# Splitting two more middle branches in a strided convolution's forward, with shared branch sums and a two-instruction cube term

## The chip, the cores and the metric

The kernel runs on one core of one Trainium2 chip. The time is that of one execution on the device, in microseconds (us). Of the kernel before there are three timed runs, 1151.36, 1152.18 and 1155.96 us (median 1152.18), and one execution taken by the profiler. TensorE (PE) multiplies matrices; its results stand in PSUM. VectorE (DVE) and ScalarE (ACT) work element by element, POOL does small copies and fills, and SP issues most transfers. Each engine works through its own queue in order.

## What is computed

```python
B, T, D, K = 2, 16000, 256, 31
s = 2
L = (T - K) // s + 1            # 7985
h = jnp.einsum('blc,cd->bld', x[:, 0:s * L:s, :], w[0])
for i in range(1, K):
    h = h + jnp.einsum('blc,cd->bld', x[:, i:i + s * L:s, :], w[i])
mu = jnp.einsum('bld->bd', h)[:, None, :] / L
var = jnp.einsum('bld->bd', (h - mu) ** 2)[:, None, :] / L
h = (h - mu) / jnp.sqrt(var + 1e-5)
h = h * gn_gamma[None, None, :] + gn_beta[None, None, :]
return _gelu(h)
```

The kernel returns this output and the gradients of `x`, `w`, `gn_gamma` and `gn_beta` for a given `grad_out`. Inputs and outputs are bfloat16.

## The kernel before

The convolution of 31 taps and stride 2 is split by phases. At each level two phase sequences and their sum replace products, so that there are three products where plain work has four. The first level has the **branches** A, B_ (the middle one) and C_, done in the order `ORDER = (B_, A, C_)`; each branch has the **leaves** A, B_ and C_ again; and the third level splits a leaf once more. A leaf can be done in two ways. `f_leaf` does it without the third split, in 24 (or 20) matmuls for each half `dh` of the outputs, a third of them 512 columns wide and the others 256. The third split does 16 matmuls on weight differences (`f_three_b` for the inner leaf, `f_outer` for both outer leaves A and C_ together) and then `f_three_ac`, four groups of eight matmuls, all 256 columns wide.

The stages follow each other on TensorE: F0 (forward of batch 0, until about 205 us), F1 (forward of batch 1, to about 414 us, with gelu of batch 0 on VectorE and ScalarE), G0 and G1 (input gradients, G0 with gelu of batch 1), and W (weight gradient). A forward has four chunks `c` of 256 positions in each of several phases; chunks two and three have c = 1 and c = 2.

For one branch, `f_sums` (its helper `tt` is L694) first adds phases: the branch sums `S`, for A and C_ only; `second` the leaf sums in one of two buffers `LL`; `third` the sums `U` for the third split. `f_mm` (L736) issues the matmuls into one of four pairs of PSUM banks, `px` and `pt`. `f_seed` writes into these banks what the branch's outer leaves are to be added onto, and `last` adds those leaves (`f_leaf` or `f_three_ac`) and takes the result out with `f_evac`, whose `keep` (L831) is a ScalarE copy, and whose squares (L864) write a scratch `JK` that nothing reads. The inner leaf of the next branch is done between `f_seed` and `last`. The set `FO` says which (batch, chunk, branch) take the third split for their outer leaves: in batch 0 all but the first middle branch, in batch 1 those of the fourth chunk. `WD` and `WD1` hold the weight differences, and `f_again` (with `w_sub`, L678) makes those of batch 1 anew. In G0 and G1, `g_sums` (L1277), `g_mm` (L1324), `g_seed` (L1385) and `g_evac` (L1395) are the counterparts, and `GU` that of `U`. `e_comp` (L1206, L1208, L1217) makes the gradient of `h` from loaded tiles. W's pairs of operands are made at L1594 to L1614 and multiplied in `w_mm` (L1528).

`gelu_unit` does one sixteenth of gelu and its derivative: ScalarE makes y and its square, VectorE the cube term z (L1101), ScalarE two sigmoids of z (L1103, L1105), and VectorE one scaling (L1107) and five products or sums (L1111).

All of SBUF is one tile, `arena`, cut by hand into buffers at byte offsets. No instruction is issued where it is written: `add` records it with its engine, inputs and outputs; `order` gives each a due time from TensorE's plan, less the amounts in the tables `lead` and `fine` (by stage, helper, caller and chunk); `listing` picks by due time among what is ready on each engine; and `emit` issues the list. So a change of a number in the tables moves instructions on every queue, and two neighbours in the code can be far apart in a queue.

## Time and profile before

| what | us |
|---|---|
| three timed runs, median | 1152.18 |
| lowest and highest of them | 1151.36, 1155.96 |
| the profiled execution | 1154.13 |
| its span, first to last instruction | 1152.4 |
| PE busy | 1122.5 |
| DVE busy | 997.9 |
| ACT busy | 532.7 |
| POOL busy | 125.4 |

The span is that of one profiled execution; its own time is 1.7 us longer. Matmuls overlap in the pipeline, so that the mean duration of one in a group is longer than the step from one to the next. L736 is line 736 of the kernel before. A wait is told as the engine and line that waited, what released it, the sum of the waits, their number and the longest. A stretch of a timeline joins instructions of one kind that follow each other, with the idle time before them in brackets.

### The profile page before, as it was taken

The numbers are of one execution on the slowest core, as the hardware profiler recorded it, in microseconds if no ns is written. First come the engines' busy times: TensorE is split into PE (matmuls) and PEld (weight loads), VectorE is DVE, ScalarE is ACT, GpSimd is POOL, SyncE is SP. The second block draws the span as 40 slices with busy tenths as digits, with TensorE's granted clock in tenths as the row PEclk, the third lists the DMA queues.
The fourth block names the chain that finished last, engine by engine and source line by source line (L and its number), as shares of the span: only waits on it lengthen the run. The fifth ranks groups of instructions, "written<-read, shape, count | busy, mean of one in ns | idle before, by whom it ended". The sixth has DMA issues, their size and how long they took to land. (4 is left out here: it accounts for less than half of the span.)

```text
span 1152.4 us, 18848 instructions
## 1 busy us (share of the span) xinstructions
PE 1122.5 (97%) x7652; PEld 749.9 (65%) x7652; DVE 997.9 (87%) x920; ACT 532.7 (46%) x817; POOL 125.4 (11%) x221
## 2 busy tenths in 40 slices
PE   5999999999999999999999899999999999999998
PEld 3888899877777874444444344444588666656785
DVE  7997787798989997999999787877799998689995
ACT  1354444768776588897744355722211212211200
POOL 0000000000000012232323223232100000000000
PEclk8999999999999999999999999999999999999999
DMA  9476657769795599999888779787997825899484
GB/s 219 69 189 119 167 156 150 171 173 203 189 232 129 203 370 267 278 274 270 225 213 189 154 203 214 201 218 147 297 293 225 305 88 167 303 296 371 146 254 119
DMA packets 345807, 243.57 MB, mean 211 GB/s; under 512 B 233377, under 2 KB 316967, under 8 KB 341543
## 3 DMA queue, kind: packets, MB, share of 16 engines
q1 hardware_dynamic: 338615, 223.47, 72.5%
q0 software_dynamic: 7104, 18.89, 5.9%
q8 instruction: 60, 0.98, 0.4%
q14 instruction: 28, 0.23, 0.1%
HBM read 106.24 MB, written 80.25 MB: 162 GB/s over the span
## 5 line engine op out<-in xcount | busy, mean ns | idle before, releaser
L736 PE MATMUL ps<-arena 128*128 128x256 bf16 (+4 forms) x3460 | 407.8, 281 | 12.4 <-DMA arena<-in_x_dram 5.5
L1324 PE MATMUL ps<-arena 128*128 128x512 bf16 x1872 | 404.5, 377 | 6.9 <-DVE arena L1277 3.4
L736 PEld LDWEIGHTS <-arena 128*128 128x128 bf16 x3460 | 338.9, 99 | 81.0 <-DMA arena<-in_x_dram 5.7
L1324 PEld LDWEIGHTS <-arena 128*128 128x128 bf16 x1872 | 183.5, 98 | 226.8 <-issue 11.4
L1528 PE MATMUL ps<-arena 128*128 128x256 bf16 (+1 forms) x2320 | 311.2, 297 | 6.5 <-DVE arena L1598 4.9
L1528 PEld LDWEIGHTS <-arena 128*128 128x128 bf16 x2320 | 227.5, 98 | 90.3 <-DVE arena L1598 5.7
L831 ACT ACTIVATE arena<-ps 128x1024 f32<-128x1024 f32 x109 | 111.0, 1022 | 262.3 <-PE ps L1528 90.1
L694 DVE TENSOR_TENSOR arena<-arena 128x2080 bf16<-128x2080 bf16 (+8 forms) x126 | 156.5, 1267 | 34.0 <-PE ps L736 33.6
L544 POOL DMA_DIRECT2D dld<-arena x144 | 104.3, 727 | 261.9 <-DMA arena<-arena 248.3
L1111 DVE TENSOR_TENSOR arena<-arena 128x2048 bf16<-128x2048 bf16 (+1 forms) x80 | 95.7, 1196 | 9.6 <-ACT arena L1103 5.3
L1277 DVE TENSOR_TENSOR arena<-arena 128x1032 bf16<-128x1032 bf16 (+1 forms) x126 | 87.5, 725 | 8.7 <-ACT arena L1226 3.3
L1496 DVE TENSOR_TENSOR arena<-arena 128x4096 bf16<-128x4096 bf16 x38 | 86.2, 2286 | 7.4 <-DMA arena<-in_x_dram 3.8
L1385 DVE TENSOR_TENSOR ps<-ps,arena 128x2048 f32<-128x2048 f32 x30 | 68.9, 2296 | 26.0 <-ACT arena L831 14.8
L1395 DVE TENSOR_TENSOR arena<-ps,arena 128x1024 bf16<-128x1024 f32 x64 | 77.0, 1218 | 8.1 <-PE ps L1324 4.8
L851 ACT ACTIVATE arena<-ps 128x512 bf16<-128x512 f32 (+1 forms) x64 | 37.1, 581 | 54.0 <-PE ps L736 53.4
L1630 ACT COPY ps<-ps 128x256 f32<-128x256 f32 x54 | 19.2, 358 | 85.2 <-PE ps L1528 84.1
L553 POOL MEMSET arena<- 128x128 bf16 (+11 forms) x40 | 8.6, 245 | 425.4 <-DVE arena L694 140.0
L1351 ACT COPY ps<-ps 128x512 f32<-128x512 f32 x48 | 27.7, 578 | 46.8 <-PE ps L1324 45.6
L1699 DVE TENSOR_TENSOR arena<-arena 128x4608 bf16<-128x4608 bf16 x16 | 40.6, 2551 | 4.7 <-PE ps L1528 4.7
L806 ACT ACTIVATE arena<-ps 128x512 f32<-128x512 f32 x56 | 29.7, 597 | 32.5 <-DVE ps L816 18.8
L772 ACT ACTIVATE ps<-ps 128x256 f32<-128x256 f32 x75 | 27.6, 369 | 34.7 <-PE ps L736 33.5
L1614 DVE TENSOR_TENSOR arena<-arena 128x2048 bf16<-128x2048 bf16 x36 | 42.8, 1218 | 0.8 <-DMA out_dram<-arena 0.8
(81 smaller groups left out, 717.1 us busy)
## 6 DMA issues: line engine op xcount, KB each, us to landing
arena<-in_x_dram SPq DMA_DIRECT2D x40, 1024.0 KB
dld<-arena POOLq DMA_DIRECT2D x144, 128.0 KB, 3.9
arena<-hd SPq DMA_DIRECT2D x32, 512.0 KB
out_dram<-arena SPq DMA_DIRECT2D x14, 1024.0 KB
arena<-dld SPq DMA_DIRECT2D x18, 640.0 KB
arena<-dld SPq DMA_DIRECT2D x18, 576.0 KB
vl<-arena SPq DMA_DIRECT2D x36, 256.0 KB
arena<-vl SPq DMA_DIRECT2D x9, 1024.0 KB
```

The lines of the kernel that those rows point to most:

```text
L544: lambda: e.dma_start(out=out, in_=in_), dma=np_ * ns / 16e3 * 1.03, ns=ns, tp=SH[pk], slack=slack)
L694: lambda: nc.vector.tensor_tensor(out=o, in0=a, in1=b, op=ALU.add))
L736: yield nc.tensor.matmul(ps[:, dh, cs], lhsT=wt, rhs=mv, start=s0, stop=False, skip_group_check=True)
L831: lambda: nc.scalar.activation(out=out, in_=ps, func=ACT.Copy, scale=scale))
L1111: add("DVE", dve(nf), [o], [a, b_], lambda: V.tensor_tensor(out=o, in0=a, in1=b_, op=op))
L1277: lambda: nc.vector.tensor_tensor(out=o, in0=a, in1=b, op=ALU.subtract))
L1324: yield nc.tensor.matmul(ps[:, e, 0:wide], lhsT=lt, rhs=mv, start=s0, stop=False, skip_group_check=True)
L1385: lambda: nc.vector.tensor_tensor(out=o, in0=x, in1=g, op=ALU.add))
L1395: lambda: nc.vector.tensor_tensor(out=ho[:, :, k, :], in0=ps[:], in1=g, op=ALU.add))
L1496: add("DVE", dve(4096), [o], [a, b], lambda: nc.vector.tensor_tensor(out=o, in0=a, in1=b, op=ALU.add))
L1528: yield nc.tensor.matmul(ps[:, s, c0:c1], lhsT=lt, rhs=mv, start=s0, stop=False, skip_group_check=True)
L1614: add("DVE", dve(2048), [o], [u, v], lambda o=o, u=u, v=v: nc.vector.tensor_tensor(out=o, in0=u, in1=v, op=ALU.subtract))
```

## The change

Four parts. The middle branch of batch 1's chunks two and three joins `FO`: its outer leaves take the third split. There its seed is made in PSUM: `f_outer`'s result is kept whole by one ScalarE copy in `TO` (half of `RB`) instead of four half copies, `f_seed` copies the inner leaf's result with its sign turned to the second bank pair, as it did before, and two VectorE instructions then add and subtract `TO` in both pairs at once. Second, there is one place for the branch sums, `S[A]`; in what was `S[C_]` the middle branch's weight differences stay alive, so that `f_again` makes those of A and C_ alone, and `U` is used anew by every branch from its first buffer, or its second for a C_ branch outside `FO`. Buffers move: `JK` now lies on part of `GU` of the middle branch, and the clearing of `DG` goes from the program's start to the start of G0. Third, the cube term takes two instructions, an addition of a constant and a product. Fourth, all numbers in `lead` and `fine` are new.

```diff
-            "F1 tt second": -38.0,
+            "F1 tt second": -162.5,
...
-    S = {A: sb(103424, 2, 2, F), C_: sb(112128, 2, 2, F)}
+    S = {A: sb(103424, 2, 2, F)}
-    U = [sb(o, 2, F) for o in (138240, 142592, 205312)]
+    U = [sb(o, 2, F) for o in (138240, 142592, 204544)]
+    TO = RB[:, 0].rearrange("p (d l f) -> p d l f", d=2, l=2)
-    JK = sb(163328, 4, HM)
-    REG = 165376
+    JK = sb(208896, 4, HM)
+    REG, EREG = 165376, 163328
-    DG, DGT = sb(209664, P), sb(209920, P)
-    ident = DGT
+    DG, DGT = sb(210176, P), sb(210432, P)
+    ident = sb(120320, P)
-    zero(DG, P)
...
-            s = S[A if b == 0 or (b, c, B_) in FO else br]
+            s = S[A]
...
+        if ts is None:
+            keep(flat2(TO), flat2(pt))
+            return
...
     def f_seed(br, px, pt, outer, ts):
         vx, vt = flat2(px), flat2(pt)
+        if outer and ts is None:
+            keep(vt, vx, -1.0)
+            for e, op in ((0, ALU.add), (1, ALU.subtract)):
+                o = bass.AP(tensor=vx.tensor, offset=vx.offset + HM * e,
+                            ap=[list(vx.ap[0]), [vt.offset - vx.offset, 2], [512, 2], [1, HM]])
+                i = TO.rearrange("p d l f -> p l d f")
+                add("DVE", dve(1024, 1), [px[:], pt[:]], [px[:], pt[:], TO],
+                    lambda o=o, i=i, op=op: nc.vector.tensor_tensor(out=o, in0=o, in1=i, op=op))
+            return
...
-    FO = {(0, c, br) for c in range(NCK) for br in ORDER if c or br != B_} | {(1, 3, br) for br in FLAST}
+    FO = {(0, c, br) for c in range(NCK) for br in ORDER if c or br != B_} | {(1, 1, B_), (1, 2, B_)} | {(1, 3, br) for br in FLAST}
...
-                tw = (WD, TS) if b == 0 else (WD1, TS1)
+                tw = (WD, TS) if b == 0 else (WD1, TS1 if c == 3 else None)
...
-                    us = {lf: U[(uc[0] + j) % (3 if outer else 2)] for j, lf in enumerate((B_, A, C_) if outer else (B_,))}
-                    uc[0] += len(us)
+                    us = {lf: U[(j + (br == C_ and not outer)) % 3] for j, lf in enumerate((B_, A, C_) if outer else (B_,))}
...
-        for br in FLAST:
+        for br in (A, C_):
...
-        add("DVE", dve(nf, 1), [z], [y2, y],
-            lambda: V.scalar_tensor_tensor(out=z, in0=y2, scalar=1.0 / GELU_A, in1=y, op0=ALU.add, op1=ALU.mult))
+        add("DVE", dve(nf, 4), [z], [y2],
+            lambda: V.tensor_scalar(out=z, in0=y2, scalar1=1.0 / GELU_A, scalar2=None, op0=ALU.add))
+        tt(z, z, y, ALU.mult)
...
-            for _ in gelu_batch(0, REG, *RINGS[0], *PACE[0]):
+            for _ in gelu_batch(0, EREG, *RINGS[0], *PACE[0]):
...
+    zero(DG, P)
```

**First place: VectorE in batch 1's second chunk.** Before, from the `third` of branch A's inner leaf (128x8x258) on; L1101 is the cube term, L1111 a gelu product, 128x8x260 a `second` of branch A. What stands behind a row is the engines whose results it waits for.

```order
L694 TENSOR_TENSOR arena<-arena 128x8x258
L1101 SCALAR_TENSOR_TENSOR arena<-arena 128x2048 [waits DVE_49,Activation_49]
L1107 TENSOR_SCALAR arena<-arena 128x2048 [waits DVE_49]
L694 TENSOR_TENSOR arena<-arena 128x8x260 [waits PE_49]
L1111 TENSOR_TENSOR arena<-arena 128x2048 [waits DMAHW4_49,DMAHW3_49,Activation_49]
```

Now, from the same `third` on; line 768 is what 694 was, 1181 what 1111 was, and 954 is the new seed add of the middle branch. The two 128x2x4x262 are the branch sums of C_.

```order
L768 TENSOR_TENSOR arena<-arena 128x8x258 [waits PE_49]
L1181 TENSOR_TENSOR arena<-arena 128x2048 [waits DVE_49]
L1190 TENSOR_SCALAR arena<-arena 128x2048
L954 TENSOR_TENSOR ps<-ps,arena 128x2x2x256 [waits Activation_49]
L768 TENSOR_TENSOR arena<-arena 128x8x260 [waits PE_49]
L1181 TENSOR_TENSOR arena<-arena 128x2048 [waits DMAHW1_49,DMAHW0_49,Activation_49]
L768 TENSOR_TENSOR arena<-arena 128x8x260 [waits PE_49]
L1181 TENSOR_TENSOR arena<-arena 128x2048 [waits DVE_49,Activation_49]
L768 TENSOR_TENSOR arena<-arena 128x2x4x262 [waits DVE_49]
L1181 TENSOR_TENSOR arena<-arena 128x2048 [waits DVE_49]
L768 TENSOR_TENSOR arena<-arena 128x2x4x262 [waits DVE_49]
L1181 TENSOR_TENSOR arena<-arena 128x2048 [waits DVE_49]
```

The second L954 is the next row. Between the two seed adds stand both `second` of branch A, leaf A first and then C_, both branch sums of C_ and four gelu products. `second` of leaf C_ waits for the f_leaf of the first chunk's branch C_, whose operand it overwrites; the `third` waits, since its `U` is now that of the middle branch.

On TensorE in the same place, the last f_leaf group of the first chunk's branch C_ (leaf C_) is followed by the four `f_three_ac` groups of branch A's inner leaf, and these by the four of the middle branch's leaf C_. The rows are the end of the former and the beginning of the latter; no other row of those four waits for VectorE.

```order
L810 LDWEIGHTS arena
L810 MATMUL ps<-arena 128x256
L810 LDWEIGHTS arena
L810 MATMUL ps<-arena 128x256 [waits DVE_49]
L810 LDWEIGHTS arena
L810 MATMUL ps<-arena 128x256
```

Before, the middle branch's leaf C_ stood there as an `f_leaf`, which waited for a ScalarE copy of the inner leaf's result alone.

**Second place: VectorE where F1 ends and G0 begins.** Before, from the last seed of the forward on; 128x2x2x258 are `third` of the input gradient's middle branch and of A, L1206 and L1208 belong to `e_comp`.

```order
L816 TENSOR_TENSOR ps<-ps,arena 128x1024
L1277 TENSOR_TENSOR arena<-arena 128x1032
L1277 TENSOR_TENSOR arena<-arena 128x2064
L682 TENSOR_TENSOR arena<-arena 128x2048
L1277 TENSOR_TENSOR arena<-arena 128x2x2x258 x2
L1206 TENSOR_SCALAR arena<-arena,stats 128x2048
L1277 TENSOR_TENSOR arena<-arena 128x1032
L1208 TENSOR_SCALAR arena<-arena,stats 128x2048
```

Now, from the `third` of A on; line 1358 is what 1277 was, 1287 and 1289 what 1206 and 1208 were.

```order
L1358 TENSOR_TENSOR arena<-arena 128x2x2x258
L1358 TENSOR_TENSOR arena<-arena 128x1032
L1358 TENSOR_TENSOR arena<-arena 128x2x516
L1358 TENSOR_TENSOR arena<-arena 128x1032
L1358 TENSOR_TENSOR arena<-arena 128x2x2x258
L1287 TENSOR_SCALAR arena<-arena,stats 128x2048
L1358 TENSOR_TENSOR arena<-arena 128x1032 x2
L1115 TENSOR_REDUCE small<-hsum_112 128x2
L1287 TENSOR_SCALAR arena<-arena,stats 128x2048
L1358 TENSOR_TENSOR arena<-arena 128x1032
L1289 TENSOR_SCALAR arena<-arena,stats 128x2048
L1358 TENSOR_TENSOR arena<-arena 128x2x2x258
```

The middle branch's `third` stood with that of A; now it is the last row, behind A's, C_'s and four `second`, and writes where the last square's scratch lies. On TensorE the middle branch's `f_three_ac` counterparts moved behind those of A and the leaf A of branch A.

432 lines of the change are left out of this document (243 added, 189 removed), and 15 rows, old and new, of the table MIR.

## Prediction

> **What bounds the kernel now.** The page comes first, for the busy shares and the chain of work that ended last; then the waits of TensorE; then the table by stretches, over the forward of batch 1 (205 to 414 us), where the change removes matmul work, and over the input gradient of batch 0 behind it.
>
> ```profile
> span 1152.4 us, 18848 instructions
> PE 1122.5 (97%) x7652; PEld 749.9 (65%) x7652; DVE 997.9 (87%) x920; ACT 532.7 (46%) x817; POOL 125.4 (11%) x221
> PE 30%; DVE 4%; DMA 3%; SPq 2%; issue 1%; ACT 0%; DVEq 0%
> PE ps L736 <- DMA arena<-in_x_dram: 5.5, 2, 4.5
> PE ps L1528 <- DVE arena L1598: 4.9, 3, 2.8
> PE ps L736 <- DVE arena L678: 4.7, 1, 4.7
> PE ps L1324 <- DVE arena L1277: 3.4, 1, 3.4
> ...
> PE ps L1324 <- DVE ps L1385: 0.5, 2, 0.3
> ```
>
> TensorE is busy in 97% of the span and leads the chain. Its waits name a place and a price: the start (5.5 and 4.7), the input gradient of batch 1 (3.4 in one piece), the weight gradient (4.9 in three). So matmul time that goes is worth its length wherever TensorE never waits, provided that nothing else turns late. The columns below are stretch, its length, then busy time and instructions of PE, PEld, DVE, ACT and POOL, the granted clock, the DMA share and GB/s.
>
> ```profile
> 205.00:257.00 52.00, 52.00 (x402) 39.01 (x401) 44.31 (x51) 37.33 (x54) 0.00 (x0) 1.00 0.74 184
> 257.00:307.00 50.00, 50.00 (x380) 36.87 (x379) 44.58 (x42) 39.07 (x60) 0.00 (x0) 1.00 0.93 209
> 307.00:357.00 50.00, 50.00 (x380) 36.86 (x379) 45.05 (x43) 38.80 (x54) 2.18 (x4) 1.00 0.75 176
> 357.00:414.00 57.00, 57.00 (x508) 49.45 (x506) 55.58 (x68) 35.64 (x73) 1.49 (x8) 1.00 0.67 211
> 414.00:470.00 56.00, 55.38 (x294) 28.51 (x292) 49.79 (x66) 49.23 (x71) 10.60 (x16) 1.00 1.04 308
> 470.00:526.00 56.00, 54.06 (x253) 24.63 (x252) 52.58 (x57) 48.37 (x57) 16.40 (x32) 1.00 1.06 277
> ```
>
> From 205 to 414 us TensorE never waits. VectorE is busy for 44.31 + 44.58 + 45.05 + 55.58 = 189.5 of 209 us, so 19.5 us are free. That small reserve is what the change draws on.
>
> **The matmuls that go.** For each of the two branches the outer leaves now take 32 matmuls on sums and 64 of the same width behind them, 96 of 256 columns, where 32 of 512 and 64 of 256 stood. The step of each width comes from two stretches in which TensorE never waits:
>
> ```profile
> 60.00:110.00 50.00, 50.00 (x459) 44.65 (x457) 41.77 (x36) 23.03 (x52) 0.00 (x0) 1.00 0.72 167
> L736 PE MATMUL ps<-arena 128*128 128x256 bf16 x300 | 36.3, 273 | 0.0
> L736 PE MATMUL ps<-arena 128*128 128x512 bf16 x80 | 20.6, 379 | 0.0
> ```
>
> From 60 to 110 us all 459 matmuls have 256 columns: 50.00 / 459 = 108.9 ns each (the 273 ns of a group is latency, since they are pipelined). The two groups are those of 307 to 357 us: (50.00 - 300 x 0.1089) / 80 = 216.5 ns for 512 columns. A branch saves 32 x (216.5 - 108.9) = 3.44 us, both save **6.9 us**, on TensorE while it is the bound.
>
> **What VectorE and ScalarE get for it.** By form, 205 to 414 us:
>
> ```profile
> L1101 DVE SCALAR_TENSOR_TENSOR arena<-arena 128x2048 bf16<-128x2048 bf16 x6 | 13.7, 2286 | 1.8 <-ACT arena L1098 1.8
> L1101 DVE SCALAR_TENSOR_TENSOR arena<-arena 128x1856 bf16<-128x1856 bf16 x2 | 4.2, 2090 | 0.0
> L1107 DVE TENSOR_SCALAR arena<-arena 128x2048 bf16<-128x2048 bf16 x6 | 4.1, 689 | 0.1
> L1107 DVE TENSOR_SCALAR arena<-arena 128x1856 bf16<-128x1856 bf16 x2 | 1.3, 638 | 0.0
> L1111 DVE TENSOR_TENSOR arena<-arena 128x2048 bf16<-128x2048 bf16 x30 | 36.6, 1221 | 4.3 <-ACT arena L1105 2.7 <-ACT arena L1103 1.3
> L1111 DVE TENSOR_TENSOR arena<-arena 128x1856 bf16<-128x1856 bf16 x10 | 11.2, 1120 | 0.0
> L694 DVE TENSOR_TENSOR arena<-arena 128x2064 bf16<-128x2064 bf16 x8 | 9.9, 1232 | 0.2 <-PE ps L736 0.2
> L816 DVE TENSOR_TENSOR ps<-ps,arena 128x1024 f32<-128x1024 f32 x8 | 9.8, 1227 | 0.0
> L678 DVE TENSOR_TENSOR arena<-arena 128x2048 bf16<-128x2048 bf16 x6 | 7.2, 1220 | 0.2 <-DMA arena<-arena 0.2
> L831 ACT ACTIVATE arena<-ps 128x1024 f32<-128x1024 f32 x8 | 8.1, 1014 | 8.2 <-PE ps L736 8.2
> ```
>
> Added to VectorE in this stage: four `third` of 1.232 and four seed adds, which the trace does not show in this form and which I price as the nearest row, the PSUM add of 1.227. Two `w_sub` of 1.220 go. Gelu's cube term, one instruction of 2.286, becomes 0.689 + 1.221, which saves 0.376 six times and, in the short form, 2.090 - 0.638 - 1.120 = 0.332 twice: 2.9 us. Together 4.93 + 4.91 - 2.44 - 2.92 = **+4.5 us**: 194.0 of 202.1 us if all of the saving came through, 8.1 free. The input gradient's stage gets 2.9 us less. ScalarE gets two `keep` of 1.014, and has room. The Trainium skill's page "VectorE: DVE Perf Modes", section "Rules for kernel authors", advises few instructions in a chain, which speaks against splitting the cube term. Taken as a count, eight more instructions in this stage would cost 8 x 0.638 = 5.1 us where the rows give a saving of 2.9. The rows decide, so this enters no term.
>
> **Where the saving is lost: one VectorE queue.** In the second chunk's middle branch the two new seed adds don't stand together. Between them stand eight instructions, among them `second` of the next branch's leaf C_, which overwrites an operand of the previous chunk's last f_leaf (branch C_, leaf C_) and so waits until its matmuls are over. Behind that point VectorE has this `second`, five more instructions and the second seed add. TensorE has four f_three_ac of eight matmuls, and then the matmuls that add onto the seed. The step of such instructions comes from the timeline, where seven of the same kinds follow each other:
>
> ```profile
> 248.31 1.24 DVE L694 TENSOR_TENSOR arena<-arena 128x2096 bf16<-128x2096 bf16 x1
> 255.17 1.24 DVE L694 TENSOR_TENSOR arena<-arena 128x2080 bf16<-128x2080 bf16 x1
> 658.54 3.78 PE L1324 MATMUL ps<-arena 128*128 128x512 bf16 x9 [3.39 <-DVE arena L1277]
> 650.00:662.00 12.00, 8.61 (x34) 3.38 (x32) 6.83 (x7) 4.99 (x8) 3.03 (x5) 0.86 1.05 205
> 1000.00:1012.00 12.00, 9.20 (x77) 7.64 (x75) 8.71 (x6) 2.62 (x4) 0.00 (x0) 0.92 1.04 377
> ```
>
> Six steps take 255.17 - 248.31 = 6.86, 1.143 each. VectorE needs 6 x 1.143 + 1.23 = 8.1 us, TensorE has 32 x 0.1089 = 3.5 us of work: it stands still for about **4.6 us**. If the first two f_three_ac need only the first seed add (it holds their columns), they fill 1.7 us more and the stall is 2.9; I take 4.6, since the order has one wait on VectorE ahead of all four and none between them. In the third chunk the two adds follow each other, with 3.04 + 2 x 3.47 + 1.74 = 11.7 us of matmuls (108 by their widths) to cover one `keep` and two adds, 1.0 + 2.4: no cost. A stall of this length also costs clock: behind the one of 3.39 us nine matmuls of 512 took 3.78 us where 9 x 0.2165 and the 0.16 us that a matmul's end lags (379 - 216.5 ns) make 2.11, so **1.7 us** were lost, and the window's clock of 0.86 says the same, 12 x 0.14. The Trainium skill, page "TensorE: Matmul & The Clock Gate", section "Part 1: The HAM clock gate", halves the clock only after an idle window of about 3.4 us, so by it a stall of 2.9 would cost no clock, and the half stall below would end 1.0 earlier. The window of 1000 to 1012 us, which holds the 2.8 of the wait on L1598, shows 0.92, a loss of 12 x 0.08 = 1.0; I go by that row.
>
> **The smaller terms.** The scratch of the squares moves onto an operand of the input gradient, so that its `third` of the middle branch now waits until ScalarE's last square is over:
>
> ```profile
> 420.70 3.62 PE L1324 MATMUL ps<-arena 128*128 128x512 bf16 x16
> 423.02 1.06 ACT L864 ACTIVATE arena<-arena 128x1024 bf16<-128x1024 bf16 x1
> L1385 DVE TENSOR_TENSOR ps<-ps,arena 128x2048 f32<-128x2048 f32 x30 | 68.9, 2296 | 26.0 <-ACT arena L831 14.8
> ```
>
> That square ends at 424.08, 3.4 us behind the forward's last matmul, and a `keep` of 1.0 may come ahead of it now. With a `third` of 0.69 TensorE can go on after 4.1 to 5.1 us; ahead of that it has 20 matmuls of 512 columns and 4 of 256, 4.8 us: +0.2 (0 to 0.5). Behind the waiting `third` stand VectorE's evacuations, whose matmuls come later. At the end of the input gradient of batch 0 a seed of 2.296 now stands behind an evacuation and a row of small instructions; between nothing and its own length I take +0.5 (0 to 2.3), nearer to nothing, since TensorE waits for L1385 for 0.5 in all now. The clearing of a 128x128 patch moves from the start to POOL's queue behind that square; POOL is busy for 10.6 of 56 us there: nothing. Loads, stores and transposes are as many as before on SP and POOL. Their order changes, as does that of the pairs in the weight gradient, where two of the three waits on L1598 (4.9 - 2.8 = 2.1) may shrink or grow: -0.5 (-2.1 to 2.1). The wait of 3.39 stays: the same three elementwise steps, which wait for loads, stand ahead of the same `second`. The stages around keep their 2.9 us of VectorE as reserve.
>
> **Sum**: -6.9 + 4.6 + 1.7 + 0.2 + 0.5 - 0.5 = -0.4 us on the profiled execution's 1154.13 (its span 1152.4 and 1.7 around it): 1153.7. The median of the runs, 1152.18, is 1.95 lower, which gives **1151.8 us**.
>
> **Rivals.** *The whole gain.* VectorE and ScalarE deliver the seed in time after all, and stall and clock (6.3) drop out: 1145.5. For it speaks that no wait of TensorE is seen in this stage; against it that eight instructions between the adds alone take 9.1 us. *Half a stall.* TensorE waits for 2.9 us and loses 1.0: 1149.4. *VectorE becomes the bound (the slower side).* Its waits in this stage:
>
> ```profile
> DVE arena L694 <- PE ps L736: 10.5, 6, 5.9
> DVE arena L1111 <- ACT arena L1105: 2.7, 1, 2.7
> DVE arena L1101 <- ACT arena L1098: 1.8, 2, 1.0
> DVE arena L1111 <- ACT arena L1103: 1.3, 3, 0.7
> ```
>
> They make 16.3 us. Free are 8.1 and, with the stall and its clock, 14.4. If all stay and the seed adds and the shared `U` (the next branch's `third` now waits for the middle branch's f_three_ac) add some 4 more, TensorE stands still for another 20.3 - 14.4 = 5.9 and loses 1.7 of clock: 1159.4. It decides from waits of over 14.4 us on. Against it: the longest, 5.9, is for a buffer that the new order frees earlier. *The gain is given back behind.* The DMA share of 1.04 and 1.06 from 414 to 526 us says that transfers set the pace there; what starts sooner then waits, in the worst case for the 6.9 less the 6.3 already lost, and new collisions of up to 2: 1154. *More goes elsewhere.* The waits at the start or in the weight gradient shrink by 3 to 6: 1146 to 1149.
>
> **How the numbers follow.** Forecast 0.38, half a stall 0.15, whole gain 0.14, VectorE bound 0.15, given back 0.10, more elsewhere 0.08. 0.5% is 5.8 us, about what a measurement can tell from no change: faster is below 1146.4, slower above 1157.9. Faster: the whole gain and most of the last, 0.20. Slower: VectorE bound and a little of the given back, 0.17. The rest, 0.63, is no change. The range reaches from the whole gain to half way into the VectorE case, **1145.2 to 1157**.
>
> **What would show it.** Right: in the forward of batch 1 the groups by form show 64 matmuls of 512 columns fewer and 64 of 256 more, and the cube term as two instructions; TensorE's waits show one of 3 to 5 us on the seed's add (L954), near 258 us, and the table by stretches a clock below 1.00 behind it; VectorE's share there is near 93%. Wrong: no such wait (then the whole gain), several of them in the two later chunks (VectorE bound), or a change of the time that lies at the start or in the weight gradient.

## The result, and the profile after

| | before | after |
|---|---|---|
| median of the runs made together, us | 1152.49 (7 runs, 1151.36 to 1156.28) | 1162.99 (7 runs, 1160.26 to 1167.65) |
| profiled execution, its span, us | 1154.13, 1152.4 | 1161.59, 1159.8 |

The ratio is 1.0082, with an interval of 1.0065 to 1.0099: the changed kernel is slower by 0.8%, where no change was forecast. Of order_of_before_joined one run, 1484.2 us at a granted clock of 0.75, is left out of the median below. The page of the changed kernel has this row of busy shares:

```profile
span 1159.8 us, 18819 instructions
PE 1116.7 (96%) x7598; PEld 751.4 (65%) x7652; DVE 997.7 (86%) x942; ACT 533.2 (46%) x819; POOL 127.6 (11%) x221
```

TensorE is busy for 5.8 us less (of 7652 matmuls, as many as before, 54 records are missing), VectorE for as long as before; the time is in TensorE's gaps. Its waits, as those of before (L810 is what L736 was, L1405 what L1324, L1609 what L1528 was):

```profile
PE ps L810 <- DMA arena<-in_x_dram: 5.8, 2, 4.7
PE ps L810 <- DVE arena L752: 4.8, 1, 4.8
PE ps L810 <- ACT ps L846: 4.4, 1, 4.4
PE ps L810 <- DVE arena L768: 3.4, 2, 1.9
PE ps L1405 <- DVE arena L1358: 3.3, 2, 3.1
PE ps L1609 <- DVE arena L1679: 3.2, 2, 2.5
PE ps L1405 <- DVE ps L1466: 2.9, 4, 2.1
PE ps L1405 <- DVE arena L1476: 2.9, 3, 2.3
PE ps L1405 <- ACT ps L1432: 1.9, 2, 1.4
PE ps L1405 <- ACT ps L908: 1.2, 1, 1.2
```

The start (5.8 and 4.8), the 3.1 of the input gradient and the 1.9 on L768 were there before. New are the 4.4 in chunk two and a crowd of waits of 0.5 to 2.5. (The 2.3 on L1476, near 532 us, costs nothing against before: three waits of 0.3, 0.9 and 0.9 us stood there.) The table by stretches puts them in two places, 257 to 307 us and 414 to 470 us (45.58 and 50.19 us busy where 50.00 and 55.38 stood):

```profile
257.00:307.00 50.00, 45.58 (x351) 35.11 (x350) 46.16 (x49) 38.24 (x56) 0.00 (x0) 0.93 0.76 173
307.00:357.00 50.00, 50.00 (x404) 39.20 (x403) 48.61 (x48) 41.56 (x59) 2.12 (x3) 1.00 0.81 194
414.00:470.00 56.00, 50.19 (x263) 26.09 (x267) 46.66 (x65) 46.17 (x68) 8.80 (x15) 1.00 0.98 301
```

To see where the time goes, the two traces are read at the points where equally much matmul work is still to be done (the steps of 108.9 and 216.5 ns summed from the end). The **lag** is the time in the one kernel less that in the kernel before. It begins near -6.9, since that much less is to be done, and ends as the difference of the two. Each column is one profiled execution, and executions differ from the start on by up to 0.7 (spliced_moved and seed_and_copies at 266 us). The columns are kernels of the experiments, the first is the changed kernel.

| time in the kernel before, us | after | seed_and_copies | chunk_two_free | order_of_before | spliced | spliced_moved | searched |
|---|---|---|---|---|---|---|---|
| 266 | -7.1 | -7.2 | -7.3 | -3.2 | -7.2 | -7.9 | -7.2 |
| 286 | -0.4 | -5.5 | -7.4 | 2.2 | -0.4 | -6.3 | -6.8 |
| 307 | -0.2 | -0.8 | 2.3 | 17.6 | -0.2 | -2.0 | -7.1 |
| 347 | -0.1 | -0.8 | 2.4 | 26.6 | -0.2 | -2.0 | -6.8 |
| 407 | -0.1 | -0.8 | 2.4 | 34.5 | 0.2 | -1.5 | 2.0 |
| 447 | 6.7 | 6.5 | 10.0 | 37.3 | 3.3 | 1.4 | 3.5 |
| 591 | 6.0 | 6.8 | 9.3 | 36.1 | 3.1 | 1.6 | 5.4 |
| 818 | 7.0 | 6.6 | 9.8 | 36.8 | 3.4 | 1.8 | 4.5 |
| 840 | 9.6 | 6.4 | 9.7 | 36.3 | 3.1 | 1.3 | 4.0 |
| 1128 | 7.9 | 8.1 | 7.7 | 37.1 | 0.8 | 1.3 | 2.3 |

So the whole gain is there at 266 us, chunk two takes 6.7 of it, the forward's end another 6.8 (0.7 of which comes back), and two places of the input gradient 2.0 (between 591 and 611 us, where batch 0 ends) and 2.6 (between 818 and 840 us, where batch 1 ends). The 2.6 belongs to this execution: in seed_and_copies and chunk_two_free, whose queues are the same there, the lag hardly moves (6.6 to 6.4, 9.8 to 9.7).

The work itself came out as priced. By form, 205 to 414 us, 64 matmuls of 512 columns fewer (288 before) and 64 of 256 more (986 before); the seed add takes what the nearest row did, and the cube term is two instructions, of 688 and 1219 ns:

```profile
L810 PE MATMUL ps<-arena 128*128 128x256 bf16 x1050 | 129.4, 276 | 4.4 <-ACT ps L846 4.4
L810 PE MATMUL ps<-arena 128*128 128x512 bf16 x224 | 57.7, 379 | 0.1
L954 DVE TENSOR_TENSOR ps<-ps,arena 128x1024 f32<-128x1024 f32 x4 | 4.9, 1227 | 0.0
L1183 DVE TENSOR_SCALAR arena<-arena 128x2048 bf16<-128x2048 bf16 x6 | 4.1, 688 | 2.1 <-ACT arena L1178 2.1
L1181 DVE TENSOR_TENSOR arena<-arena 128x2048 bf16<-128x2048 bf16 x36 | 43.8, 1219 | 7.4 <-ACT arena L1186 5.7 <-ACT arena L1188 0.9 <-ACT arena L1176 0.5
```

**Chunk two** in the timeline of the changed kernel, TensorE first, then ScalarE, then VectorE's two seed adds:

```profile
278.35 5.89 PE L810 MATMUL ps<-arena 128*128 128x256 bf16 x31 [4.35 <-ACT ps L846]
...
270.34 1.91 ACT L1186 ACTIVATE arena<-arena 128x2048 bf16<-128x2048 bf16 x1 [1.09 <-DVE arena L1181]
272.29 1.91 ACT L1188 ACTIVATE arena<-arena 128x2048 bf16<-128x2048 bf16 x1
274.10 2.36 ACT L1176 ACTIVATE arena<-arena,stats 128x1024 bf16<-128x1024 bf16 x2
...
277.92 0.39 ACT L846 ACTIVATE ps<-ps 128x256 f32<-128x256 f32 x1
...
270.83 1.23 DVE L954 TENSOR_TENSOR ps<-ps,arena 128x1024 f32<-128x1024 f32 x1
...
281.13 1.22 DVE L954 TENSOR_TENSOR ps<-ps,arena 128x1024 f32<-128x1024 f32 x1
```

TensorE stands for 4.35 us (4.6 were forecast), but what releases it is a small ScalarE copy (L846, of branch A's inner leaf), which stands behind six microseconds of gelu. The wait on the seed add (L954) that the prediction named as its sign doesn't show. The second seed add comes 10.3 us behind the first, nine steps of the prediction's 1.143; 31 matmuls behind the stall take 5.89 us where 31 x 0.1089 and 0.16 make 3.5, so the clock (0.93 in the row of 257 to 307 us, 1.00 in the next) costs 2.35 (1.7 were forecast).

**The forward's end**, TensorE with its gaps, then VectorE and ScalarE ahead of two of them:

```profile
416.82 4.53 PE L810 MATMUL ps<-arena 128*128 128x231 bf16 x44 [1.52 <-DVE arena L768]
...
446.12 1.89 PE L1405 MATMUL ps<-arena 128*128 128x512 bf16 x8 [1.43 <-ACT ps L1432]
...
413.38 1.22 DVE L756 TENSOR_TENSOR arena<-arena 128x2048 bf16<-128x2048 bf16 x1
...
415.65 2.15 DVE L768 TENSOR_TENSOR arena<-arena 128x1856 bf16<-128x1856 bf16 x2
...
443.67 1.91 ACT L1186 ACTIVATE arena<-arena 128x2048 bf16<-128x2048 bf16 x1
445.49 0.58 ACT L1432 COPY ps<-ps 128x512 f32<-128x512 f32 x1
```

The forward's last `third` (L768) stands behind a weight sum (L756) that is needed later, and a copy of 0.58 us (L1432), for which TensorE waits, behind a sigmoid of gelu. In the kernel before, the weight sum (L682) came behind the last `third` (L694), and the copy (L1351) ahead of the sigmoid (L1103):

```profile
414.21 1.12 DVE L694 TENSOR_TENSOR arena<-arena 128x1856 bf16<-128x1856 bf16 x1
...
418.31 1.23 DVE L682 TENSOR_TENSOR arena<-arena 128x2048 bf16<-128x2048 bf16 x1
...
440.45 0.57 ACT L1351 COPY ps<-ps 128x512 f32<-128x512 f32 x1 [0.25 <-PE ps L1324]
...
442.33 1.91 ACT L1103 ACTIVATE arena<-arena 128x2048 bf16<-128x2048 bf16 x1
```

Near 834 us, at the end of batch 1's input gradient, a seed (L1466) stands behind a sum of the weight gradient (L1577) that waits for a load.

```profile
830.25 2.29 DVE L1577 TENSOR_TENSOR arena<-arena 128x4096 bf16<-128x4096 bf16 x1 [2.11 <-DMA arena<-in_x_dram]
832.58 1.23 DVE L1679 TENSOR_TENSOR arena<-arena 128x2048 bf16<-128x2048 bf16 x1
833.72 2.29 DVE L1466 TENSOR_TENSOR ps<-ps,arena 128x2048 f32<-128x2048 f32 x1
...
836.07 3.53 PE L1405 MATMUL ps<-arena 128*128 128x512 bf16 x8 [2.10 <-DVE ps L1466]
```

In the kernel before the same sum (L1496) stood ahead of that seed (L1385) too, but found its load done:

```profile
822.82 2.28 DVE L1496 TENSOR_TENSOR arena<-arena 128x4096 bf16<-128x4096 bf16 x1
825.02 2.29 DVE L1385 TENSOR_TENSOR ps<-ps,arena 128x2048 f32<-128x2048 f32 x1
```

New here are a second sum (L1679) between the two and the wait for the load. That wait differs between executions: 2.11 us in this one, 0.91 in seed_and_copies and 1.02 in chunk_two_free, where TensorE's wait on the seed is 0.9 and 1.0.

### The profile page after: what moved, and what is told of

Its sections match the earlier page's. It is cut to its first block, busy times and chain, and to the rows that moved or that the text cites. A ratio compares the mean times of both kernels' runs of the same rounds, so it can differ in the third digit from the quotient of the medians.

```text
span 1159.8 us, 18819 instructions
## 1 busy us (share of the span) xinstructions
PE 1116.7 (96%) x7598; PEld 751.4 (65%) x7652; DVE 997.7 (86%) x942; ACT 533.2 (46%) x819; POOL 127.6 (11%) x221
## 5 line engine op out<-in xcount | busy, mean ns | idle before, releaser
L810 PE MATMUL ps<-arena 128*128 128x256 bf16 (+4 forms) x3460 | 403.4, 280 | 18.9 <-DMA arena<-in_x_dram 5.8
L1405 PE MATMUL ps<-arena 128*128 128x512 bf16 x1833 | 404.3, 378 | 15.4 <-DVE arena L1358 3.3
L810 PEld LDWEIGHTS <-arena 128*128 128x128 bf16 x3460 | 340.1, 99 | 82.2 <-issue 10.8
L1405 PEld LDWEIGHTS <-arena 128*128 128x128 bf16 x1872 | 183.7, 98 | 234.2 <-issue 19.6
L1609 PE MATMUL ps<-arena 128*128 128x256 bf16 (+1 forms) x2305 | 310.0, 297 | 5.2 <-DVE arena L1679 3.2
L1609 PEld LDWEIGHTS <-arena 128*128 128x128 bf16 x2320 | 227.7, 98 | 88.0 <-DVE arena L1679 3.8
L768 DVE TENSOR_TENSOR arena<-arena 128x2064 bf16<-128x2064 bf16 (+6 forms) x130 | 161.2, 1265 | 26.9 <-PE ps L810 26.5
L1181 DVE TENSOR_TENSOR arena<-arena 128x2048 bf16<-128x2048 bf16 (+1 forms) x96 | 114.6, 1194 | 12.7 <-ACT arena L1186 9.4
L1577 DVE TENSOR_TENSOR arena<-arena 128x4096 bf16<-128x4096 bf16 x38 | 86.2, 2285 | 7.7 <-DMA arena<-in_x_dram 7.4
L1476 DVE TENSOR_TENSOR arena<-ps,arena 128x1024 bf16<-128x1024 f32 x64 | 77.0, 1218 | 17.2 <-PE ps L1405 10.7
L1466 DVE TENSOR_TENSOR ps<-ps,arena 128x2048 f32<-128x2048 f32 x30 | 68.9, 2295 | 22.2 <-PE ps L1405 11.8
L846 ACT ACTIVATE ps<-ps 128x256 f32<-128x256 f32 x75 | 27.7, 369 | 44.9 <-PE ps L810 43.7
L1432 ACT COPY ps<-ps 128x512 f32<-128x512 f32 x48 | 27.8, 579 | 38.3 <-PE ps L1405 29.9
```

The costliest lines, as they stand in the source:

```text
L768: lambda: nc.vector.tensor_tensor(out=o, in0=a, in1=b, op=ALU.add))
L810: yield nc.tensor.matmul(ps[:, dh, cs], lhsT=wt, rhs=mv, start=s0, stop=False, skip_group_check=True)
L1181: add("DVE", dve(nf), [o], [a, b_], lambda: V.tensor_tensor(out=o, in0=a, in1=b_, op=op))
L1405: yield nc.tensor.matmul(ps[:, e, 0:wide], lhsT=lt, rhs=mv, start=s0, stop=False, skip_group_check=True)
L1466: lambda: nc.vector.tensor_tensor(out=o, in0=x, in1=g, op=ALU.add))
L1476: lambda: nc.vector.tensor_tensor(out=ho[:, :, k, :], in0=ps[:], in1=g, op=ALU.add))
```

## The experiments

Every instruction has a number, its place in the record that `add` makes. Most kernels here change the list that `emit` goes through, and nothing else: `(i, j, 1)` puts instruction i directly behind j, `(i, j, 0)` directly ahead of it. In the expectations, Q is the theory that the time is lost by the places of rows in the queues: each engine works through its rows in order, so a row that somebody needs stands behind rows that nobody needs yet. The other letters are rivals, of which L puts the loss on VectorE's amount of work and S, later, on the changed dependencies and the added work.

```diff
-        for i in self.order():
+        seq = self.order()
+        for i, j, behind in MOVES:
+            seq.remove(i)
+            seq.insert(seq.index(j) + behind, i)
+        for i in seq:
```

### Single rows in chunk two

983 is the second seed add and 982 the first; 961 and 987 to 989 are ScalarE rows (a result of the chunk before, and the three copies L846), 761 a gelu row of L1176. seed_only:

```diff
+MOVES = ((983, 982, 1),)
```

> The changed kernel, with one row of one queue moved: in batch 1's second chunk the second seed add (VectorE) stands right behind the first. Theory Q (the loss at this place is two queues, each of which alone makes TensorE wait: on VectorE the eight rows between the seed adds, on ScalarE squares and sigmoids ahead of the copies of branch A's inner leaf): the wait of 4.35 us near 274 us stays, between 3.9 and 4.8 us, with the clock loss behind it, and the whole time stays within 2 us of the changed kernel's. Rival D (the prediction's step: the VectorE queue alone sets it): the wait falls below 1 us and the forward of batch 1 ends 5 to 7 us earlier.

One run of 1161.53 us; the wait stays as it was, as Q had it (lines here are 7 higher than in the changed kernel):

```profile
PE ps L817 <- ACT ps L853: 4.3, 1, 4.3
```

copies_only, with the ScalarE rows ahead of the gelu row and the seed add where it was:

```diff
+MOVES = ((961, 761, 0), (987, 761, 0), (988, 761, 0), (989, 761, 0))
```

> The changed kernel, with four ScalarE rows moved: the evacuation that frees the bank of branch A's inner leaf, and the three copies behind it, stand ahead of two squares of gelu, no other row moved. Theory Q: the wait is cut in two, some 1.3 us on the first copy and some 3.5 us on the second seed add behind four f_three_ac, 4 to 5 us in all, so the place gains less than 1.5 us (at most the clock). Rival A (ScalarE alone sets it): 1.3 us in all, and the place gains 3 us and the clock, 4 to 5.5 us together.

One run of 1163.72 us. Now the seed add is what TensorE waits for:

```profile
PE ps L817 <- DVE ps L961: 3.1, 1, 3.1
PE ps L817 <- ACT ps L853: 1.6, 1, 1.6
```

Two chains of nearly one length end near the same matmuls, and taking away one shows the other. seed_and_copies makes both moves:

> Both moves together. Theory Q: one wait of 1.0 to 1.6 us is left at the place (evacuation and first copy), no clock loss; the place gains 4.5 to 5.5 us against the changed kernel, and the whole time falls from 1163.0 to about 1158. Rival L (VectorE has too much work in this stage, so what is freed here turns late a little further on): the gain is below 2 us, with new waits of TensorE between 285 and 410 us.

1160.54 us, ratio 1.0058 (1.0037 to 1.0079). The lag at 286 us is -5.5, so the stall is nearly gone there; at 307 us it is -0.8, since waits of 2.9 and 1.6 us have come up. Those are the new waits that rival L named; the gain over the changed kernel, 2.5 us, lies between the two forecasts. chunk_two_free moves the copies further ahead, and the last f_leaf of the chunk before as well:

```diff
+MOVES = ((983, 982, 1), (959, 969, 0), (961, 967, 0), (987, 967, 0), (988, 967, 0), (989, 967, 0))
```

> As the run before, and on TensorE the last f_leaf group of the first chunk's branch C_ stands ahead of the middle branch's f_three_ac, the evacuation and the copies right behind it on ScalarE. Theory Q: no wait of TensorE over 0.3 us is left at the place; it gains 6 to 7 us against the changed kernel, whole time about 1156.5; so the forward of batch 1 shows the 6.9 us of saved matmuls in full until about 405 us. Rival L: a gain below 2 us, since the same VectorE work now ends late in the third or fourth chunk.

1162.02 us, ratio 1.0081 (1.0063 to 1.0099): the whole gain at 286 us (-7.4) and more than all of it lost at 307, so that the outcome is L's. In keeps_ahead the copies of the middle branch's result, which are waited for now, also go ahead of the four gelu rows in front of them.

> chunk_two_free with one more move on ScalarE: the two copies of the middle branch's results (keep of f_evac) stand ahead of the four gelu rows that wait for VectorE, where they stood behind them; every other row of every queue stays. Theory Q: the wait of 7.3 us on that copy near 291 us goes; the gain of 7 us lasts beyond 307 us in part (lag against before of -6 to -2 there), the forward's end still costs 6.6 and the rest as in chunk_two_free: 1156 to 1160 us. Rival S: VectorE, busy for 12 of 12 us there, makes TensorE wait at the next row, the lag at 307 us is +1 to +3 as in chunk_two_free, 1161 to 1163.

1166.5 us, ratio 1.0095 (1.0075 to 1.0115). In chunk_two_free TensorE's wait and the stretch around it (the columns are those of the tables by stretches) were:

```profile
PE ps L817 <- ACT arena L915: 7.3, 1, 7.3
```

```profile
286.00:298.00 12.00, 6.43 (x31) 4.06 (x31) 11.96 (x15) 10.94 (x12) 0.00 (x0) 0.72 1.14 220
```

In keeps_ahead (lines 144 higher than the changed kernel's; L1037 is the ordinary seed add L893) they are:

```profile
PE ps L954 <- DVE ps L1037: 8.3, 1, 8.3
```

```profile
286.00:298.00 12.00, 3.65 (x15) 1.83 (x14) 11.97 (x15) 9.65 (x11) 0.00 (x0) 0.67 1.10 223
```

VectorE is busy for all of the 12 us, and TensorE waits for the next thing that it owes: with VectorE's rows in this order the rival S was right in this place, though the loss is larger than it said (a lag of 3.9 at 307 us, where it had 1 to 3), and Q's 1156 to 1160 was missed.

### More and less work

cube_held keeps the rows in their places, but for one unit in which the cube term stands a few rows later, and joins the cube term again: 16 instructions fewer, 5.8 us of VectorE more. A `tt` with None issues nothing.

```diff
-            lambda: V.tensor_scalar(out=z, in0=y2, scalar1=1.0 / GELU_A, scalar2=None, op0=ALU.add))
-        tt(z, z, y, ALU.mult)
+            lambda: V.scalar_tensor_tensor(out=z, in0=y2, scalar=1.0 / GELU_A, in1=y, op0=ALU.add, op1=ALU.mult))
+        tt(z, z, y, None)
...
```

> The changed kernel with every queue row held in its place, but gelu's cube term as one instruction of 2.29 us at the place of the first of the two, and none at the second (in one unit that place is a few rows later). 16 instructions fewer, 5.8 us more of VectorE, half of it in the forward of batch 1. Theory L (VectorE is the limit where it is busy all the time, from 270 to 300 us and where the input gradient begins): 2 to 6 us slower than the changed kernel. Theory Q (waits stand where rows stand): within 1.5 us of it.

1160.06 us, ratio 1.0055 (1.0038 to 1.0071): not slower than the changed kernel. free_lighter is chunk_two_free with one of gelu's additions left out in batch 0, so that it computes something else; VectorE is busy for 9.4 us less (988.5 where 997.9 stood):

```diff
-        tt(y2, y2, s, ALU.add)
+        tt(y2, y2, s, None if b == 0 else ALU.add)
```

> The run chunk_two_free with less work for VectorE: in gelu of batch 0 one of the five products and sums (the addition of s) is left out, eight instructions or some 9.7 us in the forward of batch 1, as much as the outer split adds there; no other row moves. Theory L: the wait of 7.3 us near 286 us falls below 2 us, the 6.9 us of saved matmuls are there until 400 us, and the whole time is 1152 to 1156. Theory Q: the wait keeps more than 4 us, since the copy that TensorE waits for stands behind the same ScalarE rows, and the whole time is above 1158.

1161.86 us, ratio 1.0067 (1.0047 to 1.0087), with a wait of 6.0 where 7.3 stood: as Q had it, 9.4 us of work less make the wait only 1.3 us shorter. before_more_work is the kernel before, in its own order, with the `third` and one `second` of the middle branch and of A in chunks two and three done three times each, 9.8 us of VectorE more:

```diff
+THRICE = (945, 1017, 982, 1054)
...
+            for _ in range(3 if i in THRICE else 1):
```

> The kernel before in its own order, with eight VectorE instructions more in the second and third chunk of batch 1, 9.8 us: two third and two second of each chunk are issued three times in a row instead of once. Nothing else changes, no matmul is saved. Theory L: VectorE has no room there, TensorE waits for 4 us or more between 255 and 360 us, and the whole time rises by 4 to 10 us. Rival R (there is room for this work in an order that suits it; the new order loses it by waits of VectorE on ScalarE ahead of the place): less than 2 us.

1157.98 us, ratio 1.0028 (1.0016 to 1.004), between the two forecasts: a third of the work reaches TensorE, as two short waits (1.6 and 1.2 us). So VectorE's amount of work is not the limit in itself: 5.8 us more cost nothing, 9.4 less won nothing that can be told from none, and the order of before hides two thirds of 9.8. It isn't without weight either: a third of the 9.8 came through.

### The numbers of one kernel in the other

after_old_numbers is the changed kernel with the tables of before, before_new_numbers the reverse; no_outer takes the two middle branches out of `FO` under the new tables.

> The changed kernel's instructions and places, ordered by the numbers (lead and fine) of before. Its two seed adds follow each other in the second chunk. Theory N (the loss comes from the new numbers, in the forward of batch 1 and where the input gradient begins): the 6.9 us of saved matmuls are there when the forward of batch 1 ends, and the whole time is 1146 to 1151 us. Rival L (VectorE's extra work in the forward of batch 1 can't be placed under TensorE whatever the order): the second or third chunk again loses 4 us or more, and the whole time is above 1155.

> The instructions and places of before, ordered by the new numbers. Theory N: the new numbers carry the loss along, 4 to 12 us slower than before, with waits of TensorE of 2 us or more in all where the forward of batch 1 ends (405 to 450 us), where before has 0. Rival L: without the new VectorE work the new numbers do no harm, within 3 us of before.

> The changed kernel without the two entries in FO: no branch of the second and third chunk takes the third split for its outer leaves, so the 6.9 us of matmuls are back and four third and four seed adds, 9.8 us of VectorE, are gone; the rest of the change stays. Rival L: no wait of TensorE is left from 260 to 310 us, so that the place's loss (6.7) and the saved matmuls (6.9) cancel: within 2 us of the changed kernel, 1161 to 1165. Theory N: the new numbers make a wait there or elsewhere in the stage all the same, 1166 or more.

They took 1254.86 us (ratio 1.0856, 1.082 to 1.0892), 1271.5 (1.0976, 1.092 to 1.1032) and 1203.89 (1.0419, 1.0382 to 1.0456). A table of these numbers fits the one set of instructions that it was made for, and loses some 50 to 110 us against the kernel before on another; as a test of the parts of the change the three failed. What they show is that the order alone, with the same instructions, is worth some 90 us (1162.99 against 1254.86). cube_joined, which joins the cube term without holding the queues, failed in the same way: the joined instruction comes under another entry of the tables, and every queue changed (1320.48 us, ratio 1.1422, 1.1378 to 1.1466).

> The changed kernel with its queues held as they are, but gelu's cube term as one instruction of 2.29 us again, at the place of the first of the two. Rival L (VectorE is the limit in the second chunk and at the begin of the input gradient): 2 to 6 us slower than the changed kernel, 1165 to 1169, most of it between 270 and 460 us. Theory Q (waits stand where rows stand, not where the work is too much): within 1.5 us of the changed kernel.

### Later places, row by row

five_moves is chunk_two_free with the weight sum (1277) behind the seed, the two sigmoids (1340, 1341) each behind one copy (so that the second copy still stands behind the first sigmoid) and two weight-gradient sums (2746, 2745) behind the seed near 834 us.

```diff
+MOVES = (..., (1277, 1238, 1), (1340, 1548, 1), (1341, 1561, 1), (2746, 2721, 1), (2745, 2721, 1))
```

> The run chunk_two_free with three more local moves: a VectorE sum for the next stage's weights behind the last branch's seeds (before 415 us), two ScalarE copies ahead of two sigmoids of gelu (445 us), and a weight-gradient sum that waits for a load behind the last seed of the input gradient (834 us). Theory Q: each gains what TensorE waits there, some 1.1, 1.4 and 1.8 us; together 3 to 5 us against chunk_two_free, 1157 to 1159. Rival L: what is moved back turns late a little later, and the gain is below 2 us.

1164.9 us, ratio 1.0092 (1.0076 to 1.0109), so L's outcome. The wait behind the weight sum went from 1.9 to 0.4 us and the one on the seed from 1.0 to 0.7; that on the copies stayed at 1.4, on the second of them; and others came up (3.1 where 1.2 stood on L915, 2.7 on L1483 behind 834 us). Moved one by one, these rows won nothing.

### One kernel's instructions in the other's order

order_of_before writes the list out: the changed kernel's instructions, each in the place of its namesake in the kernel before.

```diff
-        for i in self.order():
+        for i in SEQ:
```

> The instructions, buffers and dependencies of the changed kernel, issued in the order of the kernel before: the list is written out, each instruction in the place that its namesake had before; the new ones (f_outer, third, seed adds, f_three_ac of the two branches) stand where the f_leaf, seed and third of that branch stood, and the few that the shared branch sums and U forbid there (f_sums of branch C_, third of C_'s inner leaf) stand at the first place that they allow. Theory Q (what is lost is lost by the places that rows have in the queues): chunk two and the forward's end give up most of the +6.7 and +6.6, so 1146 to 1151 us, and no wait of TensorE at the forward's end. Rival S (what is lost is lost by the changed dependencies and the extra work: one place for branch sums, the shared U, 4.5 us more of VectorE in the forward): the waits come back at other rows, 1155 us or more, with waits of TensorE of 4 us or more together from 257 to 310 us.

> As order_of_before, with gelu's cube term as one instruction again (2.29 us instead of 0.69 and 1.22, sixteen times: 16 instructions fewer, 5.8 us more of VectorE). Theory Q: within 2 us of order_of_before either way. Rival S (VectorE's work counts): 3 to 6 us slower than order_of_before.

1191.26 us (ratio 1.0306, 1.028 to 1.0332) and, with the joined cube term, 1189.91 (4 runs; 1.0301, 1.0278 to 1.0323). Q's 1146 to 1151 was far off, and S's side came: from 266 to 407 us that order loses 38 us. But the column of lags tells more. From 447 us to the end the lag stays between 35 and 39 and ends where it began (37.3, 37.1): **behind the forward the old order loses nothing in the end**, where the changed kernel's own order loses 4.6 at two places. And at the forward's end there is the wait on the squares' scratch that was forecast, a `third` of the input gradient (L1502 here) behind ScalarE's last square (L1085), and TensorE behind it:

```profile
458.66 0.70 DVE L1502 TENSOR_TENSOR arena<-arena 128x1032 bf16<-128x1032 bf16 x1 [1.14 <-ACT arena L1085]
...
459.42 2.77 PE L1549 MATMUL ps<-arena 128*128 128x512 bf16 x12 [1.46 <-DVE arena L1502]
```

spliced takes the changed kernel's order up to its 1160th entry (the start of the last chunk, where the two lists hold the same instructions but one) and the order of before from there.

> The changed kernel's own order up to the start of the forward's last chunk (its first 1160 entries), and from there the same instructions in the order of the kernel before, as in order_of_before. Where order_of_before lost nothing (everything behind the forward but for 2.8 us at its end, where a third of the input gradient waited for the last square), this one should lose nothing either. Theory Q (the forward's end and the input gradient's seeds lose 6.6 + 2.0 + 2.6 by the new numbers alone): lag against before near 0 until 409 us, +2 to +3 at the forward's end, none at the two seeds: 1155 to 1158 us, some 5 to 8 below the changed kernel. Rival S (the losses there follow from what the forward leaves behind, so that they return whatever the order): 1161 us or more.

1155.03 us (12 runs, 1153.12 to 1158.75; ratio 1.0022, 1.0009 to 1.0035), as Q had it: 0.6% below the changed kernel's 1.0082, which is 6.9 us, and 7.1 by the last row of the lags. Its longest wait of TensorE from 400 to 470 us:

```profile
PE ps L1549 <- DVE arena L1502: 1.5, 1, 1.5
```

The chunk-two stall is unchanged in it (lag -0.4 at 286 us), so the 7 us are what the new order lost from the forward's last chunk on, about half of it by 447 us (a lag of 3.3, not 6.7). spliced_moved adds the moves of seed_and_copies, takes two rows of gelu out of the way of VectorE's next sigmoid, and brings two rows forward at the forward's end.

> spliced with the moves of seed_and_copies in chunk two and three more places: on ScalarE two rows of gelu that make y for the next unit go behind the two sigmoids and the copies that stood behind them, so that VectorE's wait of 4.3 us near 232 us on the first sigmoid is 2 us shorter; at the forward's end one matmul group of branch A and one step of the gradient of h go ahead of those that wait for the last square. If VectorE's idle time ahead of chunk two is what is late there, the lag at 307 us falls from -0.8 (seed_and_copies) to about -3, and the forward's end costs 1 less: 1151 to 1154 us. If not, the lag at 307 us stays near -0.8: 1154 to 1157.

1154.91 us (12 runs, 1153.25 to 1157.24; ratio 1.0008, 0.9995 to 1.0021): level with the kernel before. The lag at 307 us is -2.0, between the two cases, but 0.7 of its 1.2 below seed_and_copies stands already at 266 us. VectorE's wait on that sigmoid fell from 4.3 to 2.0 us, and about 0.5 of it reached TensorE, whose waits there are 2.5 and 1.6 us where 2.9 and 1.6 stood. searched puts the rows of all three engines in two stretches in a new order.

> spliced_moved with the rows of TensorE, VectorE and ScalarE put in another order in two stretches, 206 to 345 us (chunks one to three of the second forward) and 395 to 470 us (its end and the beginning of the input gradient); the instructions, the buffers and SP's and POOL's queues stay. The order was searched by working out each row's start from the durations and the dependencies seen in spliced_moved's trace; worked out so, its waits of TensorE from 270 to 345 us go (it has 4.1 us there in the trace), and those of 410 to 430 us (3.6 us) shrink to about 1. Theory Q (the dependencies allow the whole gain, only the order loses it): lag against before of -6 to -7.5 at 345 us and of -5.5 to -7 at 470, and 1146 to 1150 us at the end unless the later stages, whose queues aren't touched, give some back. Rival S (the one place for branch sums and the shared U cost a wait that no order takes away): lag of -2 or more at 345 us, 1153 us or more.

1159.5 us (12 runs, 1155.81 to 1162.39; ratio 1.0036, 1.0021 to 1.0051). TensorE's timeline from 236 us on, and then in the last chunk:

```profile
236.22 37.72 PE L954 MATMUL ps<-arena 128*128 128x256 bf16 x288 [1.17 <-ACT ps L990]
274.21 70.99 PE L954 MATMUL ps<-arena 128*128 128x256 bf16 x572 [0.28 <-DVE ps L1098]
```

```profile
352.09 14.12 PE L954 MATMUL ps<-arena 128*128 128x256 bf16 x89 [5.14 <-ACT ps L990]
...
344.68 1.15 ACT L1320 ACTIVATE arena<-arena,stats 128x928 bf16<-128x928 bf16 x1
...
350.07 0.36 ACT L990 ACTIVATE ps<-ps 128x256 f32<-128x256 f32 x1
```

From 236 to 345 us TensorE stands still for 0.28 us, and the lag is -6.8 at 347: the shared branch sums, the shared `U` and the added VectorE work do allow the whole gain through chunks two and three. S fell there. The two stretches around the point where that ends:

```profile
307.00:345.00 38.00, 38.00 (x314) 30.45 (x312) 36.05 (x36) 26.89 (x40) 2.30 (x3) 1.00 0.67 179
345.00:370.00 25.00, 19.86 (x134) 13.83 (x133) 23.38 (x26) 21.04 (x31) 0.47 (x2) 0.86 1.01 214
```

Where the searched stretch ends, a copy of 0.36 us stands behind rows of gelu (L1320 among them) that the search had left ahead of it, and 5.1 us of wait and 2.3 of clock take the gain away in one place. At 475 us, just behind the second searched stretch, TensorE waits another 2.2 us for a copy. Whether an order exists that keeps it to the end of the forward is open: VectorE was busy for 36.05 of 38 and 23.38 of 25 us there, so little of it is free.

## Why the prediction was wrong, step by step

- **The matmuls that go, -6.9.** Right: 64 and 64 matmuls, and a lag of -7.1 at 266 us.
- **VectorE's and ScalarE's new work.** Right in size (1227 ns for the seed add). The rival in which VectorE becomes the bound by its waits came nearest in time (1159.4), but not by its mechanism: its sign, several waits in the two later chunks, didn't come, and cube_held and free_lighter speak against the amount of work.
- **The stall in chunk two, 4.6, and the clock, 1.7.** Right in place and size, 4.35 and 2.35 (at 274 us, where 258 was said), and half right in mechanism. The seed add was late as described (copies_only: 3.1 us on it alone), but a second chain on ScalarE, not named, had the same length and was what TensorE waited for; so the size fits in part by luck. The sum, forecast at 6.3, was 6.7. The 1.0 of clock behind the stall of 2.80 us, used for half a stall, is a misreading: the window of 1000 to 1012 us ends 2.5 us behind that stall, and 1009 to 1021 us has 0.86, so 12 x 0.14 = 1.7. Half a stall would come to 1150.1 by it; the forecast stays.
- **The third chunk, the loads, POOL, the clearing.** The chunk is right: no wait of TensorE from 307 to 400 us. POOL and the clearing too: TensorE waits for neither. The loads were priced at nothing, and one of them, by the sum near 830 us, delays a seed.
- **The smaller terms: this is the step that failed.** It priced the forward's end at +0.2, for the one wait that the new place of the scratch makes, and a seed where the input gradient of batch 0 ends at +0.5, and it had no term for the end of batch 1's. Measured were 6.8 (0.7 of it came back), 2.0 and, in this execution, 2.6. The named wait was harmless in the changed kernel, which had moved the matmuls behind it, and costs 1.5 us where they weren't moved (order_of_before, spliced). The step looked for waits that new dependencies make. What cost was the order without any new dependency: at the forward's end a weight sum ahead of a `third` and sigmoids ahead of copies, which stood the other way round before. spliced, the same instructions in the old order there, gives 7 us of it back. What is shown is the order as a whole; how much of it is due to which row isn't, since five_moves won nothing. The late seed at 834 us is a mixed case: one sum stood ahead of it before as well; new are a second sum between them, which is order again, and the wait for a load, whose length varies between executions.
- **The weight gradient, -0.5.** The lag goes from 8.6 to 7.9 from 861 us to the end, -0.7: right, but by luck. It rises to 10.5 by a wait of 2.5 us on L1679 near 873 us, falls to 6.7 by 1020 us, since the wait of 2.8 and its clock are gone there, and rises by 1.2 again. The prediction held the 2.8 fixed and let only the two shorter waits vary.

By the lags, the sum reads -7.1 + 6.7 + 0.3 + 6.8 - 0.7 + 2.0 - 1.0 + 2.6 - 1.0 - 0.7 = 7.9 (the spans differ by 7.4), where -0.4 was forecast; the terms not named above (0.3, and -1.0 twice) are what the lag drifts between the places. The rival in which the gain is given back behind the forward had the place right, but blamed transfers, which bear on 834 us alone, and stopped at 1154.

## What to carry to other kernels

Where a change comes with a new order, each engine's queue has to be read row by row at every stage boundary, not only where the work changes: for each row that TensorE waits for, what stands ahead of it, and does that wait for somebody. A stall that has one name may be two chains of the same length, and moving one row at a time then wins little; splicing one kernel's order onto the other's at a point where both lists hold the same instructions told in one run which half had lost the time. A loss read from one execution is to be looked for in others with the same rows there: that of the forward's end is in all of them, that at 834 us only in some. Numbers that steer a scheduler can't be swapped between two versions as an experiment.

## What was not expected of the hardware

Splitting the cube term saves VectorE 0.38 us each time (2286 ns against 688 and 1219; 0.33 in the short form), 5.8 us in all, and no run shows any of it in the time: 1.0055 joined against 1.0082 split, as ratios to the kernel before, in one order, 1189.91 us against 1191.26 in another. The Trainium skill, page "VectorE: DVE Perf Modes", section "Rules for kernel authors", advises for chained operations not to fuse for speed and to keep their number small. The first half agrees with these durations; of the second the runs show nothing, since the one instruction takes longer than the two and the whole time doesn't tell them apart.

And the clock that a stall costs grows little with its length once it is long: 2.35 us behind 4.35, and, from the lags less the waits, 2.3 behind 5.14 (searched), 2.4 behind 7.3 (chunk_two_free) and 2.9 behind 8.3 (keeps_ahead). Shorter stalls cost about 1.7 or nothing, and not by their length alone. Behind the one of 3.39 us in the kernel before it was 1.7. Behind the changed kernel's 2.10 at 836 us 8 matmuls of 512 columns take 3.53 us where 8 x 0.2165 and 0.16 make 1.9, so 1.6 are lost, and the granted clock from 836 to 848 us is 0.86. Behind the 3.12 of copies_only 80 matmuls of 256 take 8.93 us where 80 x 0.1089 and 0.16 make 8.9, nothing lost, at a clock of 1.00. The Trainium skill, page "TensorE: Matmul & The Clock Gate", section "Part 1: The HAM clock gate", has the clock halved for about 3.4 us of work after an idle window of about 3.4 us, a loss of 1.7 as an estimate from it. The loss agrees where there is one, up to 1.2 above; as a bound for the idle time the 3.4 does not, since 2.10 us were enough here.
